# Cosine attention and a GELU layer: one scale and its transposing DMA moved ahead of a square

## The chip, the core and the metric

The kernel runs on one core of a Trainium2 chip. Time is device microseconds of one execution; lower is better. The core has five engines that run side by side, each with a queue of its own that is worked off in order: PE (matrix multiply), DVE (vector), ACT (activation functions), POOL (GpSimd) and SP (here it only issues transfers). Transfers run on 16 DMA engines that all queues share. A transfer that SP issues goes into SP's hardware queue (q1 in the profile); one that POOL issues goes into the software queue (q0).

## The reference

```python
q_n = q / (norm(q, axis=-1) + 1e-6)          # q, k, v: (8 batches, 12 heads, 448, 64)
k_n = k / (norm(k, axis=-1) + 1e-6)
scores = q_n @ k_n.T / tau                   # tau = 0.1
attn = exp(scores - max); attn /= sum(attn)
x = (attn @ v) -> (3584 tokens, 768)         # heads side by side
h = x @ w_in                                 # 768 x 2048
g = 0.5 * h * (1 + erf(h / sqrt(2)))         # exact GELU
out = g @ w_out                              # 2048 x 768
```

All inputs and the output are float32.

## The kernel before

**Tiling.** Four heads of one batch make a quad; a batch has three quads (`NQ = 3`), so there are 24. A quad is computed at a time: its q and k lie as `qk` [128, 2 (q, k), 2 (head pairs), 7, 64] in float32. For each quad the kernel squares q and k (`square`, line 140, POOL), sums the squares of each row (`reduce`, 151, DVE), takes logarithm and exponential of a half for the root (`logs` 162 and `roots` 167, ACT), adds 1e-6 and takes the reciprocal (`inverses`, 176, POOL then DVE for the quad of this change), multiplies q and k by it into bfloat16 (`scale`, 193, two POOL instructions), and turns the result so that the head dimension lies on partitions (`transposes`, 207). For the first batch's quads the turning is done by PE and copied by DVE; from the second batch on it is one transposing DMA issued by SP (line 213).

**Attention.** `scores` (227) multiplies k by q into `st`, `exps` (238) takes the exponential on ACT, `sums` (247) and `values` (261) are PE's row sums and products with v. The sums are turned into a factor on DVE (`turned` 275, `inverted` 280, `spread` 296), and `normalise` (301) multiplies it into `x`, one of six slices of 64 x 2 columns for each call. The last two slices of a batch come from its quad 2.

**The two layers.** `first(b)` (595) is the first layer of a batch with its GELU: 16 tiles `hp` of six contraction steps each, 96 matmuls (line 607), each tile finished by a GELU on ACT (638). The first five tiles start with four steps each (`ahead`), which need only the slices of quads 0 and 1; the other two steps need the slices of quad 2. The tiles take turns on the PSUM banks of attention: two double banks and two single ones, each free again when its GELU has read it. The second layer (`second_pieces`, 323) is cut into single matmuls that the next batch's attention uses as filling between its scores.

**What sets the order.** Everything is issued in an order written out by hand, under `manual_schedule`; each engine runs its part of it in that order, and waits are put in for data and buffers. `attention_first` (385) is the first batch, line by line; `done` counts for each step how many units have been issued, and `upto(f, n)` issues those that are missing. Unit numbers run over the quads with the first quad cut in two, so that unit 4 is quad 0 of the second batch, 5 its quad 1 and 6 its quad 2. Units 5 and 6 share one root, so that `root(5)` needs the squares and sums of both.

**Around the change.** Before, `attention_first` ends with `inverses(4)`, behind the last two slices of `x`. Then `first(0)` issues, behind the first 20 matmuls (lines 617 to 619):

```python
        if b == 0:
            upto(square, nu + 3)
        for n in (nu + 1, nu + 2) if b else (nu + 1,):
            upto(scale, n)
            upto(transposes, n)
```

With `nu = 4` these are the square of unit 6, the scale of unit 4 and its transposing DMA. Next come two loads of `wo` (`load_wo`, issued by POOL), the sums of squares of units 5 and 6, and the 16 GELUs. After the sixth GELU ACT changes its table and works out the root of units 5 and 6 (line 641); POOL then scales both and SP issues their transposing DMAs, with loads of `qk` between. At the end of `first(0)`, `group(1, 0)` issues the first scores of the second batch, which read what the DMA of unit 4 wrote.

Of the kernel before, what the change touches and what calls it, by code (L numbers as in the profile page):

```python
# [16 lines left out]
def kernel(  # L17
# [78 lines left out]
    def mm_tile(name, shape=(128, 512), dtype=F32, aside=None):  # L96
        t = ps_mm.tile(list(shape), dtype, tag=f"mm{turn[0] if aside is None else turn[0] ^ aside}", name=name)
        if aside is None:
            turn[0] ^= 1
        return t  # L100
# [75 lines left out]
    def inverses(n):  # L176
        sr = sr_t.pop(n)
        shape = [128] + shapes[n]
        se = nrm.tile(shape, F32, tag="se", name=f"se{n}")
        if n <= NQ:  # L180
            nc.vector.tensor_reduce(se.rearrange("p j i s c -> p (j i s c)"), sr, mybir.AxisListType.X, ALU.add)
        else:
            nc.gpsimd.tensor_scalar(se, sr, 1e-6, None, ALU.add)  # L183
        rn = nrm.tile(shape, F32, tag="rn", name=f"rn{n}")
        nc.vector.reciprocal(rn, se)  # L185
        rn_t[n] = rn
# [6 lines left out]
    def scale(u, parts=None):  # L193
        g, s0, s1 = units[u]
        n, j = place[u]
        rn = rn_t[n][:, j]
        if g not in qkb_t:
            qkb_t[g] = qkbp.tile([128, 2, C, 2, D], BF16, tag="qkb", name=f"qkb{g}")
        qkb, t = qkb_t[g], qk_t[g]
        for eng, i in parts or ((nc.gpsimd, 0), (nc.gpsimd, 1)):  # L200
            eng.tensor_tensor(  # L201
                qkb[:, i, :, s0:s1].rearrange("p c s d -> p s c d"), t[:, i, s0:s1],
                rn[:, i].to_broadcast([128, s1 - s0, C, D]), ALU.mult)
# [3 lines left out]
    def transposes(u, i=None):  # L207
        g, s0, s1 = units[u]
        qkb = qkb_t[g]
        if g not in qkT_t:  # L210
            qkT_t[g] = qkTp.tile([128, 2, C, 128], BF16, tag="qkT", name=f"qkT{g}")
        if i is None:
            nc.sync.dma_start_transpose(out=qkT_t[g].rearrange("p i c s -> p (i c) s"),
                                        in_=qkb.rearrange("p i c s d -> p (i c s d)"))
            return
        tp = tp_t[u, i] = mm_tile(f"tp{u}_{i}", (128, C, 128), BF16)
        for c in range(C):
            nc.tensor.transpose(tp[64 * s0:64 * s1, c, :], qkb[:, i, c, s0:s1].rearrange("p s d -> p (s d)"), ident)  # L218
# [42 lines left out]
    def values(g, chunks=range(C), aside=None):  # L261
        for c in chunks:
            if c == 0:
                bank_t[g, 0] = ps_acc.tile([128, 512], F32, tag="o", name=f"o{g}_0")
                bank_t[g, 1] = mm_tile(f"o{g}_1", aside=aside)
            for s in range(2):
                for h in range(2):
                    rows, cols = slice(64 * h, 64 * (h + 1)), slice(64 * s, 64 * (s + 1))
                    nc.tensor.matmul(bank_t[g, h][cols, :S], lhsT=v_t[g][rows, s, c, :],  # L269
                                     rhs=pt_t[g, s, c][rows], start=(c == 0), stop=(c == C - 1),  # L270
                                     tile_position=(64 * h, 64 * s))
# [8 lines left out]
    def inverted(g):  # L280
        tr = bank_t.pop((g, "tr"))
        if g < NQ:
            su = tr[:, :, :, 0]
        else:


            for j in range(4):
                o = j ^ 1
                nc.vector.tensor_reduce(tr[32 * j:32 * (j + 1), :, :, 1], tr[32 * o:32 * (o + 1), :, :, 0:1],  # L289
                                        mybir.AxisListType.X, ALU.add)  # L290
            su = rcp.tile([128, 2, NB], F32, tag="su", name=f"su{g}")
            nc.vector.tensor_reduce(su, tr[:, :, :, 0:2], mybir.AxisListType.X, ALU.add)
        rc = bank_t[g, "rc"] = rcp.tile([128, 2, NB], F32, tag="rc", name=f"rc{g}")
        nc.vector.reciprocal(rc, su)

    def spread(g, h):
        rs = rcp.tile([128, NB, 32], F32, tag=f"rs{h}", name=f"rs{g}_{h}")
        nc.vector.transpose(rs, bank_t[g, "rc"][:, h].to_broadcast([128, NB, 32]))  # L298
        rs_t[g, h] = rs.rearrange("p b r -> p (b r)")

    def normalise(g, h):
        b, n = divmod(g, NQ)
        nc.vector.tensor_tensor(x_t[b][:, 2 * n + h, :], bank_t.pop((g, h))[:, :S], rs_t.pop((g, h)), ALU.mult)  # L303
# [68 lines left out]
    done = {}  # L372
# [12 lines left out]
    def attention_first():  # L385
# [154 lines left out]
        roots(4)  # L540
        inverted(2)
        spread(2, 0)
        values(2, (2,))
        values(2, (3,))
        values(2, (4,))
# [2 lines left out]
        normalise(2, 0)  # L548
        spread(2, 1)
        normalise(2, 1)  # L550
        inverses(4)
        done.update({square: 6, reduce: 5, root: 5, scale: 4, transposes: 4})

    passes = [(n, c) for n in range(NQ) for c in range(C)]

# [105 lines left out]
    for b in range(B):  # L661
        if b == 0:
            attention_first()
        else:
            attention(b, fill)
        first(b)
        sb, hf = divmod(b, 2)
        todo = [(t, ni) for t in (range(3) if hf == 0 else range(3, 7)) for ni in range(2)]
        if b == 0:
            todo.sort(key=lambda x: x[1])  # L670
        tail = [2 * S // 128 - 1] if b == B - 1 else []
        fill = [f for t, ni in todo if t not in tail for f in second_pieces(sb, t, ni)]
        fill += [f for t in tail for f in last_pieces(sb, t)]
# [37 lines left out]
```

## Time and profile before

| what | us |
|---|---|
| time, median of 7 | 430.2 (427.87 to 433.18) |
| the profiled execution | 427.87 |
| its span, first to last instruction | 425.9 |
| PE busy | 414.7 (97%) |
| ACT busy | 247.4 (58%) |
| DVE busy | 191.6 (45%) |
| POOL busy | 166.4 (39%) |

The granted TensorE clock is full over the whole span. Times in the views are counted from the first instruction, so they fit into the span; what the time has over it lies around the span. In a timeline a line gives start, length, engine, line of the kernel, operation, what it writes and reads, and how many of one kind were merged; brackets hold the idle time before it and what ended it. The page's list of transfers gives 4.0 us as the median of the transposing DMAs from issue to landing, over 21 of them.

### The profile page before, as it was taken

The page shows a single profiled execution, that of the slowest core. Times are in us where ns is not written, and L with a number is a line of the kernel's source. Part 1 is how long each engine was busy: PE and PEld are TensorE (multiplying, and loading weights), DVE is VectorE, ACT ScalarE, POOL GpSimd, SP SyncE. Part 2 cuts the span into 40 slices and gives each one's busy share as a digit, 9 for nine tenths or more (in the row PEclk, how much of TensorE's full clock was granted, in tenths as well). Part 3 has the DMA queues.
Part 4 walks back from the last instruction along what each step waited for, and adds up shares of the span by engine and source line. Part 5 has one row for each costly group of instructions (what it writes and reads, how often), then busy time and mean ns, then how long its engine had stood idle before and what let it go on. Part 6 is the DMA issues. An engine that isn't in the chain of part 4 may idle for free.

```text
span 425.9 us, 8166 instructions
## 1 busy us (share of the span) xinstructions
PE 414.7 (97%) x3448; PEld 208.5 (49%) x3448; DVE 191.6 (45%) x379; ACT 247.4 (58%) x356; POOL 166.4 (39%) x113
## 2 busy tenths in 40 slices
PE   7899879999999999999999999999999999999996
PEld 3444434555454554545454544555544455445564
DVE  6897017840288304941167501971048611562021
ACT  5895758546655467734767348745666357754300
POOL 5798606360813509090540906353180622000000
PEclk9999999999999999999999999999999999999999
DMA  8999999482492805655092642938076320320023
GB/s 287 270 251 204 190 232 261 97 201 76 84 210 51 229 33 104 168 118 180 17 218 73 133 164 24 239 74 232 2 120 186 82 43 2 82 56 20 2 74 75
DMA packets 68340, 54.99 MB, mean 129 GB/s; under 512 B 40400, under 2 KB 63312, under 8 KB 68304
## 3 DMA queue, kind: packets, MB, share of 16 engines
q1 hardware_dynamic: 55808, 42.25, 37.7%
q0 software_dynamic: 12112, 11.80, 18.0%
q8 instruction: 27, 0.44, 0.4%
q10 hardware_dynamic: 384, 0.43, 0.3%
q14 instruction: 9, 0.07, 0.1%
HBM read 45.61 MB, written 11.01 MB: 133 GB/s over the span
## 4 chain that ended last, share of the span: by engine, by line
PE 90%; DMA 4%; POOL 3%; issue 2%; ACT 0%; DVE 0%; POOLq 0%
PE op L332 35%; PE hp L607 31%; PE st L234 9%; PE o L269 8%; PE sm L258 4%; DMA qkT<-qkb 4%; POOL qkb L201 2%; PE op L347 1%; POOL wi L361 1%; PE sm L253 1%; POOL sq L149 1%; ACT g L638 0%; POOL v L134 0%; PE tp L218 0%; DVE last L350 0%
## 5 line engine op out<-in xcount | busy, mean ns | idle before, releaser
L241 ACT ACTIVATE pt<-st 128x896 bf16<-128x896 f32 x168 | 145.0, 914 | 51.8 <-PE st L234 51.6
L332 PE MATMUL op<-wo,g 128*128 128x384 bf16 x864 | 151.5, 327 | 0.0
L607 PE MATMUL hp<-x,wi 128*128 128x448 bf16 x768 | 146.7, 353 | 0.0
L638 ACT ACTIVATE g<-hp 128x448 bf16<-128x448 f32 x128 | 66.5, 545 | 95.5 <-PE hp L607 95.2
L332 PEld LDWEIGHTS <-g 128*128 128x128 bf16 x864 | 79.3, 98 | 66.9 <-issue 19.1
L607 PEld LDWEIGHTS <-wi 128*128 128x128 bf16 x768 | 74.5, 98 | 71.5 <-issue 2.9
L201 POOL TENSOR_TENSOR qkb<-qk,rn 128x896 bf16<-128x896 f32 (+1 forms) x48 | 77.9, 1649 | 9.2 <-DVE rn L185 9.2
L149 POOL TENSOR_TENSOR sq<-qk 128x1792 f32<-128x1792 f32 (+2 forms) x23 | 67.8, 2950 | 15.1 <-DMA qk<-in_k_dram 14.8
L336 DVE COPY ot<-op 128x384 f32<-128x384 f32 x54 | 29.6, 548 | 89.4 <-PE op L332 89.4
L183 POOL TENSOR_SCALAR se<-sr 128x28 f32<-128x28 f32 (+1 forms) x14 | 4.4, 312 | 167.0 <-ACT sr L174 167.0
L158 DVE TENSOR_REDUCE nq<-sq 128x28 f32<-128x1792 f32 (+2 forms) x30 | 48.7, 1633 | 27.3 <-POOL sq L149 27.2
L234 PE MATMUL st<-qkT 64*64 64x448 bf16 x672 | 52.9, 361 | 4.2 <-DMA qkT<-qkb 3.3
L185 DVE RECIPROCAL rn<-se 128x28 f32<-128x28 f32 (+2 forms) x18 | 6.9, 386 | 89.4 <-POOL se L183 89.2
L269 PE MATMUL o<-pt,v 64*64 64x448 bf16 x672 | 37.8, 352 | 0.0
L234 PEld LDWEIGHTS <-qkT 64*64 64x64 bf16 x672 | 17.6, 104 | 34.0 <-issue 24.7
L298 DVE STREAM_TRANSPOSE rs<-rc 128x448 f32<-128x448 f32 x48 | 28.2, 624 | 0.8
L303 DVE TENSOR_TENSOR x<-o,rs 128x448 bf16<-128x448 f32 x48 | 27.0, 598 | 0.4 <-PE o L269 0.2
L269 PEld LDWEIGHTS <-v 64*64 64x64 bf16 x672 | 18.3, 106 | 17.2 <-issue 9.1
L277 DVE STREAM_TRANSPOSE tr<-sm 128x448 f32<-128x448 f32 x24 | 15.5, 647 | 11.7 <-PE sm L258 11.1
L258 PE MATMUL sm<-pt,ones 128*32 128x448 bf16 x294 | 19.6, 355 | 0.0
L289 DVE TENSOR_REDUCE tr<-tr 32x28 f32<-32x28 f32 x84 | 16.5, 196 | 1.6
L258 PEld LDWEIGHTS <-ones 128*32 128x32 bf16 x294 | 6.9, 95 | 10.1 <-issue 6.6
(44 smaller groups left out, 117.8 us busy)
## 6 DMA issues: line engine op xcount, KB each, us to landing
out_dram<-ot SPq DMA_DIRECT2D x54, 192.0 KB, 2.7
qk<-in_q_dram SPq DMA_DIRECT2D x23, 448.0 KB, 5.7
qk<-in_k_dram SPq DMA_DIRECT2D x23, 448.0 KB, 6.4
v<-in_v_dram POOLq DMA_DIRECT2D x7, 672.0 KB, 9.6
wi<-in_moe_w_in_dram POOLq DMA_DIRECT2D x8, 384.0 KB, 10.5
wo<-in_moe_w_out_dram POOLq DMA_DIRECT2D x4, 768.0 KB, 14.1
qk<-in_q_dram SPq DMA_DIRECT2D x2, 224.0 KB, 3.5
v<-in_v_dram POOLq DMA_DIRECT2D x1, 448.0 KB, 7.9
```

The costliest lines, as they stand in the source:

```text
L149: eng.tensor_tensor(sq[:, part], t[:, part], t[:, part], ALU.mult)
L158: nc.vector.tensor_reduce(nq[:, part], sq[:, part], mybir.AxisListType.X, ALU.add)
L201: eng.tensor_tensor(qkb[:, i, :, s0:s1].rearrange("p c s d -> p s c d"), t[:, i, s0:s1], rn[:, i].to_broadcast([128, s1 - s0, C, D]), ALU. ...
L234: nc.tensor.matmul(st[cols, n, :S], lhsT=qkT[rows, 1, c, cols], rhs=qkT[rows, 0, :, cols], start=True, stop=True, tile_position=(64 * s, 6 ...
L241: nc.scalar.activation(pt[:, :m], st[:, :m, :S], AF.Exp, scale=inv_tau)
L258: nc.tensor.matmul(bank_t[g, "sm"][r:r + 32, :S], lhsT=ones, rhs=pt_t[g, s, c], start=(c < 2), stop=(c >= C - 2), tile_position=(0, r))
L269: nc.tensor.matmul(bank_t[g, h][cols, :S], lhsT=v_t[g][rows, s, c, :], rhs=pt_t[g, s, c][rows], start=(c == 0), stop=(c == C - 1), tile_po ...
L298: nc.vector.transpose(rs, bank_t[g, "rc"][:, h].to_broadcast([128, NB, 32]))
L332: nc.tensor.matmul(ps[:, :NH], lhsT=g_t[sb][:, kf, t * 128:(t + 1) * 128], rhs=wo[:, kf, ni * NH:(ni + 1) * NH], start=(kf == 0), stop=(kf ...
L336: nc.vector.tensor_copy(ot[:, ni * NH:(ni + 1) * NH], ps[:, :NH])
L607: nc.tensor.matmul(hps[m], lhsT=wi[:, kd, m * 128:(m + 1) * 128], rhs=x_t[b][:, kd, :], start=(kd == 0), stop=(kd == KD - 1))
L638: nc.scalar.activation(g_t[sb][:, m, hf * S:(hf + 1) * S], hps.pop(m), AF.Gelu)
```

## The change

The reciprocal of unit 4 goes up, ahead of the last two slices of `x`; the scale of unit 4 and its transposing DMA go with it, and so come ahead of the square of unit 6 on POOL. `first(0)` then finds them issued and leaves them out. Nothing else moves and nothing that is computed changes.

```diff
         roots(4)
         inverted(2)
         spread(2, 0)
+        inverses(4)
+        scale(4)
+        transposes(4)
         values(2, (2,))
         values(2, (3,))
         values(2, (4,))
...
         normalise(2, 0)
         spread(2, 1)
         normalise(2, 1)
-        inverses(4)
-        done.update({square: 6, reduce: 5, root: 5, scale: 4, transposes: 4})
+        done.update({square: 6, reduce: 5, root: 5, scale: 5, transposes: 5})
```

## The prediction

> **What bounds the kernel now.** First the page's busy shares: PE 97% of a 425.9 us span, DVE 45%, ACT 58%, POOL 39%. The change moves POOL, DVE and SP work only, so it can pay only where PE stands still. Hence the waits of PE next: its longest is one wait of 3.3 us of the scores (`st`, line 234) for `qkT`, and no other after the start-up is over 0.3 us. The chain that ended last goes through the same place:
>
> ```profile
> 38.58 1.91 ACT g L638 x5
> 40.48 14.98 DMA qkT<-qkb
> 55.51 0.57 PE st L234 x8
> ```
>
> Start, length, piece. One transposing DMA, here called T4 (quad 0 of the second batch), takes 14.98 us to land, and the scores start the moment it has. The timeline of PE shows the size of the gap:
>
> ```profile
> 33.83 18.33 PE L607 MATMUL hp<-x,wi 128*128 128x448 bf16 x96
> 55.51 0.57 PE L234 MATMUL st<-qkT 64*64 64x448 bf16 x8 [3.35 <-DMA qkT<-qkb]
> ```
>
> The 96 matmuls of the first layer end at 33.83 + 18.33 = 52.16; 3.35 us are idle. Afterwards PE has no wait of size to the end, so what is saved here reaches the end, and 3.35 us is the most there is. What releases T4 is in the timeline of POOL:
>
> ```profile
> 33.63 0.28 POOL L183 TENSOR_SCALAR se<-sr 128x28 f32<-128x28 f32 x1 [0.95 <-ACT sr L174]
> 33.99 3.17 POOL L149 TENSOR_TENSOR sq<-qk 128x1792 f32<-128x1792 f32 x1
> 37.12 3.33 POOL L201 TENSOR_TENSOR qkb<-qk,rn 128x896 bf16<-128x896 f32 x2
> 40.40 1.85 POOL L368 DMA_DIRECT2D wo<-in_moe_w_out_dram  x2
> ...
> 44.38 6.62 POOL L201 TENSOR_TENSOR qkb<-qk,rn 128x896 bf16<-128x896 f32 x4 [0.62 <-DVE rn L185]
> ```
>
> Square of quad 2 (3.17), then the two scales of quad 0, done at 40.45; T4 is issued 0.03 later. SP's queue is otherwise idle then.
>
> **Part 1: the reciprocal moves up on DVE.** DVE's timeline:
>
> ```profile
> 33.91 0.65 DVE L298 STREAM_TRANSPOSE rs<-rc 128x448 f32<-128x448 f32 x1
> 34.66 0.62 DVE L303 TENSOR_TENSOR x<-o,rs 128x448 bf16<-128x448 f32 x1
> ...
> 35.94 0.62 DVE L303 TENSOR_TENSOR x<-o,rs 128x448 bf16<-128x448 f32 x1
> 36.48 0.32 DVE L185 RECIPROCAL rn<-se 128x28 f32<-128x28 f32 x1
> ```
>
> The reciprocal (0.32) now follows the first spread (33.91 + 0.65 = 34.56). Its input `se` is there at 33.63 + 0.28 = 33.91, so it adds no wait: it runs from about 34.60 to 34.92. Behind it are two `x`, a spread and the reduces. The last `x` goes from 36.56 to 36.9. Who waits: the first layer's last two contraction steps. PE starts at 33.83 with five tiles of four steps, 20 matmuls of 18.33 / 96 = 0.191, so it asks for these `x` at 37.65. Cover 0.75 us: cost nothing. Without cover it would be 0.33 us.
>
> **Part 2: POOL's order.** `se` still ends at 33.91. POOL now idles until the reciprocal: 34.92 plus 0.09 (the later pair, 43.79 + 0.50 to 44.38) = 35.0. Scales 3.33: done at 38.34; T4 issued at 38.37, **2.11 us earlier**. The square follows, 38.34 to 41.5, 4.3 us later than before; the two `wo` issues run 41.5 to 43.35, 1.1 later. The software queue has `wo`'s first half and a `v` load ahead of these, so their packets start no later (that queue never empties between 30 and 59 us), and PE needs that half of `wo` only after 48 matmuls, at about 66.
>
> **Part 3: what is late because the square is late.** Reduce of quad 2 on DVE waits for the square: 41.5 + 1.98 = 43.5. The logarithm on ACT waits for it, and ACT's GELUs are queued behind:
>
> ```profile
> 42.70 0.34 ACT L165 ACTIVATE lq<-nq,tiny 128x56 f32<-128x56 f32 x1
> ...
> 44.64 2.43 ACT L638 ACTIVATE g<-hp 128x448 bf16<-128x448 f32 x5
> 47.66 0.54 ACT L638 ACTIVATE g<-hp 128x448 bf16<-128x448 f32 x1 [0.59 <-PE hp L607]
> ```
>
> ACT had nothing to wait for at 42.70; now it starts at 43.55, 0.85 late. The five GELUs end at 47.92 instead of 47.07. The fifth frees the bank of the thirteenth tile, which PE starts at 33.83 + 72 x 0.191 = 47.57: PE stalls 0.35 to 0.4 us, and the first layer ends at about 52.55. That lies inside the gap while T4 lands later; if T4 came first it would be paid. It puts the ceiling of the gain at 55.51 - 52.55 = 2.95 us. The exps of the new scores wait for a table load (1.28 after the last GELU, so to 54.4), with 3.1 us of second-layer matmuls between, so they hold nobody.
>
> **Part 4: how long T4 takes.** Two things make it slow, seen in the DMA view for 43 to 44.5 us, then for 44.5 to 46 us (packets, MB, share of 16 engines; q0 is the software queue, q1 SP's):
>
> ```profile
> q0 software_dynamic: 361, 0.29, 123.7%
> ...
> q1 hardware_dynamic: 3, 0.00, 0.4%
> ```
>
> ```profile
> q0 software_dynamic: 217, 0.19, 94.0%
> q1 hardware_dynamic: 188, 0.05, 37.8%
> ```
>
> T4's packets start only at about 44.5, 4.0 us after its issue, and from then go one for one with the software queue's. A transposition at 85.66 with nothing beside it begins within 1.3 us and lands after 4.0. Here is a rule to weigh: the Trainium skill, DMA: Bandwidth & Descriptors, "Latency and other measured facts", puts the first byte of a hardware-generated DMA at some 600 ns. By it (an estimate) T4 would start at 39.0, be through before PE is, and the gain would be the ceiling, 2.95. By the row it starts at 38.37 + 4.0 = 42.4, amid the same `wo` packets. I take the row: same DMA, same traffic, 2 us apart.
>
> From there it needs as long as before, except that it meets more of `v`: what went by between about 43.4 and 44.5, some 200 packets (q0 moved 361 in 1.5 us). From 49 to 52 us, beside `wo`, q1 moved 560 packets, 187 per us; beside `v` 171 (46 to 47), or 144 over 44.5 to 47 with an instruction fetch in it. So 200 x (1/171 - 1/187) = 0.1 to 200 x (1/144 - 1/187) = 0.3; I take 0.2. Landing: 55.46 - 2.11 + 0.2 = 53.55, so the scores start **1.9 us** earlier.
>
> **Part 5: the next transposition, T5 (quad 1).** Issued at 47.74, it landed 13.6 us later, 61.3; PE asks for it some 8.3 us after the first scores, so before at 63.8, now at 61.9. Its scale is 0.85 later, issue 48.6. Kept at 13.6 it lands at 62.2, 0.3 late; but it queued behind T4, which is now 2 us sooner out of the way, and the total bytes are the same, so about 61. I take no cost; ends 0 and 0.3.
>
> **Sum**: 425.9 - 1.9 = 424.0 of span; with 427.87 - 425.9 = 2.0 around it, 426.0 for the profiled execution. That one was the fastest of those shown, 2.3 under the median, so on the median 430.2 - 1.9 = **428.3**. Bounds of the likeliest: start delay 3.1 to 4.5, hence gain 2.95 down to 1.2, that is 427.25 to 429.0.
>
> **Rivals.**
> A fuller release: T4's late start came of the `wo` issues on POOL at 40.40, or of what was already in the engines then, and is shorter at 38.4. For it: the 1.3 us of the quiet case. Against: loads of later batches beside a `v` stream also start late (at 117.72 one is issued, by 120.8 one packet is out). Gain 2.95: 427.25.
>
> No gain: T4 started just as the first half of `wo` ran out; if that is what it waits for, issuing sooner changes nothing. For: the coincidence at 44.5. Against: the later loads beside `v` start before that stream ends. Time 430.2 + 0.1 (more `v` beside it): 430.3.
>
> Slower: the late square. Through reduce and logarithm it blocks ACT, whose GELUs free PE's banks. With ACT d us late the first layer ends at 52.16 + (d - 0.5); this decides from d = 3.85 (first layer past 55.5) and costs over 0.5% from d = 6.0. My d is 0.85; POOL's scales at their longest row (2.58 instead of 1.67 each) make it 2.7. So it needs some 3.5 us of delay on POOL or DVE that no row shows. At d = 6.4: 432.6.
>
> **How the numbers follow.** Likeliest 0.55, fuller release 0.20, no gain 0.11, slower 0.14. 0.5% is 2.15 us, about what a measurement of this kernel can tell from no change, and the likeliest case lies next to it: of its 0.55 I give 0.26 to faster, 0.28 to same, 0.01 to slower. Fuller release: 0.19 and 0.01. No gain: 0.08 same, 0.03 slower. Slower: 0.13, and 0.01 same. Sums 0.45, 0.38, 0.17. The range reaches past the fuller release by half a microsecond of spread between runs, and past no gain into the slower case: 426.7 to 431.2; the likeliest's own is above.
>
> **What would show it.** Right: T4 issued near 38.4, landing near 53.5 (some 15 us); scale pair at 35.0; square at 38.3; the logarithm at 43.5; PE's wait for `qkT` near 1 us after a first layer ending at 52.5; no wait of PE for T5. Wrong: a landing after 55 in spite of the early issue; a wait before 37.65 for `x`; PE waiting for banks by more than 0.5 us; a new wait of the scores at 61 to 62.

## The result, and the profile after

The changed kernel takes **426.98 us** in the median (426.29 to 431.51, 27 runs), the kernel before, in the same comparison, 429.65 us (64 runs); the ratio is **0.9945, 95% interval 0.9931 to 0.996**, a gain of 2.4 us (1.7 to 3.0). The profiled executions differ by less: spans 425.9 and 424.4, 1.5 us. That gap between 1.5 and 2.4 is the interesting part, and the profiles of before and after alone don't explain it.

PE's wait for the transposing DMA went from 3.3 us to 1.5, and there is a second, short one now. The timeline of PE places them:

```profile
33.51 18.55 PE L609 MATMUL hp<-x,wi 128*128 128x448 bf16 x96
53.55 0.57 PE L234 MATMUL st<-qkT 64*64 64x448 bf16 x8 [1.48 <-DMA qkT<-qkb]
...
62.19 0.38 PE L234 MATMUL st<-qkT 64*64 64x448 bf16 x4 [0.26 <-DMA qkT<-qkb]
```

This execution reached the first layer 0.32 us sooner than the one before (33.51, not 33.83), which is start-up and not the change; so times are compared from the first layer's start. The first scores come 20.04 us behind it instead of 21.68: 1.64 won at T4. The second half of the scores that used to be one piece at 63.51 now waits for T5, and the matmuls behind it start 62.50 - 33.51 = 28.99 behind the layer's start, where it was 64.01 - 33.83 = 30.18: 1.19 is left. T5 took back 0.45. The 1.19 and the 0.32 of start-up are the 1.5 us between the two spans.

POOL, in the new order:

```profile
33.31 0.28 POOL L183 TENSOR_SCALAR se<-sr 128x28 f32<-128x28 f32 x1 [0.95 <-ACT sr L174]
34.54 3.33 POOL L201 TENSOR_TENSOR qkb<-qk,rn 128x896 bf16<-128x896 f32 x2 [0.95 <-DVE rn L185]
37.84 3.17 POOL L149 TENSOR_TENSOR sq<-qk 128x1792 f32<-128x1792 f32 x1
40.96 1.84 POOL L368 DMA_DIRECT2D wo<-in_moe_w_out_dram  x2
```

It idles 0.95 us for the reciprocal, scales, and squares afterwards. T4 is issued at 37.90. On DVE the reciprocal and the two slices of `x` behind it:

```profile
34.17 0.28 DVE L185 RECIPROCAL rn<-se 128x28 f32<-128x28 f32 x1
34.75 0.62 DVE L303 TENSOR_TENSOR x<-o,rs 128x448 bf16<-128x448 f32 x1 [0.29 <-DVE rn L185]
...
36.03 0.62 DVE L303 TENSOR_TENSOR x<-o,rs 128x448 bf16<-128x448 f32 x1
```

The last `x` is there at 36.65; PE asks for it at 33.51 + 20 x 0.191 = 37.33. ACT:

```profile
43.09 0.34 ACT L165 ACTIVATE lq<-nq,tiny 128x56 f32<-128x56 f32 x1 [0.71 <-DVE nq L158]
...
45.03 2.86 ACT L640 ACTIVATE g<-hp 128x448 bf16<-128x448 f32 x6
```

The logarithm now waits 0.71 us for the late sum, and the GELUs come that much later; PE's first layer takes 18.55 us instead of 18.33.

T4's start is in the DMA view for 41 to 42 and for 42 to 43 us, SP's queue (packets, MB, share of the 16 engines):

```profile
q1 hardware_dynamic: 9, 0.00, 1.7%
```

```profile
q1 hardware_dynamic: 180, 0.05, 34.9%
```

It starts at 42.0, again 4.1 us after its issue. It lands 15.6 us after it (53.5), and T5 14.0 us after its own (62.1).

### The profile page after: what moved, and what is told of

Read it like the earlier page. It is cut to its first block, busy times and chain, and to the rows that moved or that the text cites. A ratio compares the mean times of both kernels' runs of the same rounds, so it can differ in the third digit from the quotient of the medians.

```text
span 424.4 us, 8166 instructions
## 1 busy us (share of the span) xinstructions
PE 414.8 (98%) x3448; PEld 208.6 (49%) x3448; DVE 191.7 (45%) x379; ACT 247.3 (58%) x356; POOL 166.4 (39%) x113
## 4 chain that ended last, share of the span: by engine, by line
PE 86%; POOL 5%; DMA 3%; issue 2%; DVE 2%; ACT 0%; POOLq 0%
PE op L332 33%; PE hp L609 30%; PE st L234 9%; PE o L269 8%; PE sm L258 4%; DMA qkT<-qkb 3%; POOL qkb L201 3%; POOL sq L149 1%; PE op L347 1%; DVE nq L158 1%; POOL wi L361 1%; PE sm L253 0%; DVE x L303 0%; POOL v L134 0%; DVE rn L185 0%
## 5 line engine op out<-in xcount | busy, mean ns | idle before, releaser
L149 POOL TENSOR_TENSOR sq<-qk 128x1792 f32<-128x1792 f32 (+2 forms) x23 | 67.8, 2950 | 15.1 <-DMA qk<-in_k_dram 14.9
L234 PE MATMUL st<-qkT 64*64 64x448 bf16 x672 | 53.1, 361 | 2.5 <-DMA qkT<-qkb 1.7
L269 PEld LDWEIGHTS <-v 64*64 64x64 bf16 x672 | 18.3, 106 | 17.2 <-issue 9.1
L289 DVE TENSOR_REDUCE tr<-tr 32x28 f32<-32x28 f32 x84 | 16.5, 196 | 1.6
```

The costliest lines, as they stand in the source:

```text
L149: eng.tensor_tensor(sq[:, part], t[:, part], t[:, part], ALU.mult)
L234: nc.tensor.matmul(st[cols, n, :S], lhsT=qkT[rows, 1, c, cols], rhs=qkT[rows, 0, :, cols], start=True, stop=True, tile_position=(64 * s, 6 ...
```

## The experiments

### E1: the reciprocal alone

```diff
         spread(2, 0)
+        inverses(4)
         values(2, (2,))
...
         normalise(2, 1)
-        inverses(4)
```

> Only the reciprocal of unit 4 moves up (part 1 of the prediction); scale and transposing DMA stay behind the square. My theory: the last slice of x is 0.33 us later, inside a cover of 0.75 us, so PE's 96 first-layer matmuls start and end as before and T4 is issued as before: ratio 1.000, within 0.2%. Rival (the reciprocal itself helps or hurts, by what DVE or POOL does around it): a ratio off 1.000 by more than 0.3%, with a gap in the first layer, or a POOL row that moved.

Measured: 429.47 us, ratio 0.9992 (0.9973 to 1.001). The reciprocal by itself costs and wins nothing: DVE idles 0.29 us behind it as in the changed kernel, and the first layer takes 18.33 us. But this profile showed what the first two had not. PE:

```profile
55.18 0.57 PE L234 MATMUL st<-qkT 64*64 64x448 bf16 x8 [3.49 <-DMA qkT<-qkb]
55.69 4.78 PE L332 MATMUL op<-wo,g 128*128 128x384 bf16 x18
```

and the same kernel by stretches (window, length, busy time and number for PE, PE's loads, DVE, ACT, POOL, then the granted clock, DMA share, GB/s):

```profile
54.00:56.00 2.00, 0.82 (x10) 0.35 (x11) 0.00 (x0) 0.38 (x1) 0.00 (x0) 1.00 1.29 191
56.00:58.00 2.00, 2.00 (x9) 0.98 (x7) 0.00 (x0) 1.34 (x2) 0.00 (x0) 0.53 1.27 191
58.00:60.00 2.00, 2.00 (x10) 0.94 (x8) 0.00 (x0) 0.00 (x0) 0.00 (x0) 0.62 1.32 164
```

Behind the wait for T4 the TensorE clock falls to little over half for some 4 us (0.53 and 0.62). The 18 matmuls take 4.78 us, where they took 3.10 in the profile before: 1.7 us that no wait shows.

### E2, E3: the second half of `wo` loaded behind all three scales

Before and changed kernel, each with:

```diff
-        else:
-            upto(load_wo, 4)
...
                     upto(scale, n)
                     upto(transposes, n)
+                if b == 1:
+                    upto(load_wo, 4)
```

> The kernel before with the second half of wo loaded later: its two loads are issued behind the three scales and transposing DMAs instead of ahead of them. My theory (T4 is slow because its packets alternate with the software queue's): T4 is still issued at 40.4 and still starts about 4 us later, but from about 48 us on it is alone and lands near 51.5, before the first layer ends at 52.2; PE's 3.35 us wait goes without the change: ratio about 0.992. T5, issued into a quiet queue, lands about 4 us after its issue. Rival (the latency is the transposing DMA's own here, or that of the first one): T4 lands 15 us after issue again, ratio 1.000.

> The changed kernel with the same later loads. My theory: T4 lands near 50 us, so the first layer sets the scores, at about 52.4 (the late square costs PE 0.2 us): the change is worth nothing any more, ratio 0.992 to 0.993 to the kernel before and equal to the other kernel with late loads within 0.2%. Rival (the change pays through something else than T4's landing): still some 0.5% faster than that kernel.

Measured: E2 425.78 us, ratio 0.9908 (0.9886 to 0.9929); E3 427.14 us, 0.994 (0.9919 to 0.9961). In neither profile does PE wait for T4 at all. T5, issued when the software queue had all but run dry, landed 4.0 us after its issue in E2 and 4.1 in E3: the 14 us of the other kernels are not the transposing DMA's own. The price of loading so late is seen in E3's timeline of PE:

```profile
35.87 18.55 PE L611 MATMUL hp<-x,wi 128*128 128x448 bf16 x96
54.36 0.57 PE L234 MATMUL st<-qkT 64*64 64x448 bf16 x8
...
70.74 1.46 PE L332 MATMUL op<-wo,g 128*128 128x384 bf16 x8 [0.85 <-DMA wo<-in_moe_w_out_dram]
```

and in E2's profile PE waits for `wo` twice, by 7.3 us together. But that profile is of the longest of E2's six executions, 438.23 us, which the ratio leaves out; how long the other executions waited there isn't known.

Neither profile is a clean pair with the kernel before, since both reach the first layer late: E2's at 37.89, with the clock at 0.66 from 10 to 20 us, E3's at 35.87 at full clock. T4 landed 7.4 us after its issue in E2 and 12.8 in E3, but E2's was issued at 44.55, by when the loads ahead of it were further along, and E3's landing at 53.1 missed the 50 that I had expected, by more than the late start of 2.0 us. The 0.3% between E2 and E3, which I had expected to be 0.2% at most, isn't explained. So the two show for T5 that a quiet software queue takes the delay away; for T4 a better place for `wo` was needed (E7, E8).

### E4: the square of unit 6 twice

```diff
         if b == 0:
             upto(square, nu + 3)
+            square(nu + 2)
```

> The changed kernel with the square of unit 6 done twice (same values again), which puts 3.17 us more on POOL between T4's scales and everything behind. This prices the slower rival (late square, late logarithm, GELUs late, PE without banks). My sum: logarithm 4.0 us later than in the kernel before, first layer ends 3.5 us later, at about 55.7, while T4 still lands at 53.5; the scores start about as in the kernel before: ratio 1.000 (0.998 to 1.002). Were POOL's lateness hidden, it would stay at 0.9945; were it paid in full twice, 1.005.

Measured: 429.79 us, ratio 0.9995 (0.9972 to 1.0017). PE:

```profile
33.38 13.79 PE L609 MATMUL hp<-x,wi 128*128 128x448 bf16 x72
50.48 6.31 PE L609 MATMUL hp<-x,wi 128*128 128x448 bf16 x24 [3.31 <-ACT g L641]
56.72 0.57 PE L234 MATMUL st<-qkT 64*64 64x448 bf16 x8
```

The chain of part 3 is there as predicted: the thirteenth tile waits 3.31 us for a GELU, and the scores wait for the first layer and no more for T4. The ratio came out as summed, but partly by luck, since the sum lacked a term: the clock fell in this wait too (0.59 from 50 to 52 us, 0.56 from 52 to 54), so that the last 24 matmuls took 6.31 us and the scores started at 56.7, where 55.7 had been expected; and behind the scores, where E1 lost its time to the clock, this kernel lost none.

### E5: the kernel before, a second profile

> The kernel before itself, for a second profile: the one of before is of an execution at 427.9 us, while most lie near 429.5. The first set suggests why: with a wait of 3.49 us for T4 the granted TensorE clock fell to 0.53 to 0.62 for some 4 us and 18 matmuls took 4.78 us instead of 3.10. Theory (clock drop): a typical execution of the kernel before shows PE's wait for T4 again at 3.3 to 3.5 us, and behind it a clock near 0.55 and 1.7 us lost. Rival (T4 lands later in the typical execution): a wait of about 5 us and a clock of 1.00.

This one execution took 430.58 us. PE's timeline and two of its stretches:

```profile
55.39 0.96 PE L234 MATMUL st<-qkT 64*64 64x448 bf16 x8 [3.28 <-DMA qkT<-qkb]
56.29 5.52 PE L332 MATMUL op<-wo,g 128*128 128x384 bf16 x18
```

```profile
56.00:58.00 2.00, 2.00 (x10) 0.86 (x7) 0.00 (x0) 1.73 (x2) 0.00 (x0) 0.50 1.27 191
58.00:60.00 2.00, 2.00 (x8) 0.89 (x7) 0.00 (x0) 0.00 (x0) 0.00 (x0) 0.50 1.33 151
```

T4 was issued at 40.44 and landed 14.9 us later, and PE waited 3.28 us, as in the first profile (40.48, 15.0, 3.35). The rival, a later landing, is out for this execution. What differs is the clock: 18 matmuls in 5.52 us instead of 3.10 and the scores in 0.96 instead of 0.57, 2.8 us in all. The times of the kernel before say how often: of the 64, 12 lie at 428.1 or under and 52 at 428.9 or over. The profile that the prediction was made from (427.87) is one of the 12. That the two groups are the clock's doing is seen in the mean clock of each execution. E1's profiled execution, with its one fall, has 0.996, E5's longer fall makes 0.992, and the first profile has 1.000. Of the 32 executions of the kernel before that were timed beside E6b, the five at 427.9 or under have a mean clock of 1.000; of the 27 at 429.1 and over, 26 have 0.996 or less and one has 1.000.

### E6: dummy matmuls in the wait

```diff
             nc.scalar.preload_act_table_set(EXP_SET)
+            if b == 0:
+                spin(8)
             group(b + 1, 0)
```

> The kernel before with eight dummy matmuls (results unused) ahead of the first scores of the second batch, inside the wait for T4, so that PE never stands still for over 3 us. Nothing else moves. Theory (clock drop): T4 lands as before and the wait's end stays, but the clock stays at 1.00: the 1.7 us go in the executions that had them, median near 427.8, ratio 0.995 to 0.997. Rival (the clock has no part in it): ratio 1.000.

Measured: 428.07 us, ratio 0.9946 (0.9925 to 0.9966); five of six executions at 427.7 to 428.5, with mean clocks of 0.999 and 1.000. The one that was profiled is the sixth, 429.43, with 0.996:

```profile
51.82 1.68 PE L383 MATMUL spin<-blank,ident 128*128 128x448 bf16 x8
55.41 0.57 PE L234 MATMUL st<-qkT 64*64 64x448 bf16 x8 [1.91 <-DMA qkT<-qkb]
55.91 4.78 PE L332 MATMUL op<-wo,g 128*128 128x384 bf16 x18
```

Even with only 1.91 us of standing still the clock fell (0.69 from 56 to 58 us, 0.50 from 58 to 60). So the wait was filled further, with `spin(13)` in the kernel before (E6b) and, by the same edit, `spin(4)` in the remaining wait of the changed kernel (E6c):

> The kernel before with thirteen dummy matmuls in the wait for T4 instead of eight: they fill it up to about 54.6, so that less than 1 us of standing still is left. In the profile with eight of them 1.91 us were left and the clock still fell to 0.50. Theory (the clock falls on too little work in a stretch of a few us, not only on a full stop of 3.3): no execution falls any more, median 427.5 to 427.8, ratio 0.994 to 0.996, all executions within 1 us; scores still start at 55.4. Rival (a fall there comes at random, whatever PE does): part of the executions still at 429.4.

> The changed kernel with four dummy matmuls in its remaining wait of 1.5 us. Theory: its executions at 428 and above are those in which the clock fell in this wait; they go, the others stay at 426.3 to 427.3, so median about 426.6, ratio 0.9925 to 0.994, and 1.0 to 1.3 us below the kernel before with the wait filled, which is what the earlier landing of T4 is worth without the clock. Rival (the whole gain of the change is the clock): equal to the kernel before with the wait filled.

Measured: E6b 427.86 us, ratio 0.9967 (0.9949 to 0.9986), 20 of 22 executions at 427.3 to 428.5 with mean clocks of 0.998 and over; E6c 426.81 us, ratio 0.9941 (0.992 to 0.9962), all 11 at 426.4 to 428.0. E6b's two others are at 432.3 and 432.7 (0.984 both); the profile fell on one of these:

```profile
57.38 2.62 PE L383 MATMUL spin<-blank,ident 128*128 128x448 bf16 x13
60.35 0.57 PE L234 MATMUL st<-qkT 64*64 64x448 bf16 x8 [0.35 <-DMA qkT<-qkb]
60.86 3.10 PE L332 MATMUL op<-wo,g 128*128 128x384 bf16 x18
```

All of it is 5 us late, and most of that is the clock, which had fallen in the start-up (0.59 over 10 us is, by estimate, 4 us):

```profile
10.00:20.00 10.00, 8.43 (x41) 3.33 (x41) 7.33 (x13) 6.76 (x10) 4.68 (x6) 0.59 1.15 278
```

At the wait itself it holds: 3.10 us for the 18. The rival (falls at random) is out for this place: none of 22 lies between 428.6 and 432, where the kernel before has the bulk of its executions.

E6c against E6b is the change with the clock taken out: 426.81 to 427.86, **1.05 us** (1.1 by the two ratios). E6b against the kernel before (429.71 in this comparison) is the clock: **1.85 us** between the medians; by the ratio, which counts the two late executions in, 1.4 us (0.6 to 2.2). E6c's profile has T5's wait of 0.69 us in it:

```profile
53.59 0.57 PE L234 MATMUL st<-qkT 64*64 64x448 bf16 x8 [0.64 <-DMA qkT<-qkb]
54.09 3.10 PE L332 MATMUL op<-wo,g 128*128 128x384 bf16 x18
...
62.66 0.38 PE L234 MATMUL st<-qkT 64*64 64x448 bf16 x4 [0.69 <-DMA qkT<-qkb]
```

### E7, E8: the second half of `wo` between the scales of units 5 and 6

The cause points to a better kernel: give the transposing DMAs a quiet queue, and load the weights in time all the same. In the kernel before (E7) and the changed one (E8):

```diff
-        else:
-            upto(load_wo, 4)
...
                 upto(scale, nu + 2)
                 upto(transposes, nu + 2)
+                upto(load_wo, 4)
                 upto(load_qk, 2 * NQ + 1)
```

> The kernel before with the second half of wo issued between the scale of unit 5 and that of unit 6, so earlier than in the kernel with late loads, where PE waited for wo. Theory: T4 starts 4 us after its issue at 40.4, has no wo beside it from about 48 us on and lands by 52; no wait of PE for T4 and none for wo: ratio 0.990 to 0.991. Rival (wo's packets come back soon enough to slow T4): a wait of over 1 us left, ratio 0.994.

> The same place for wo in the changed kernel. Theory: T4 lands before the first layer ends, and the change has nothing left to win; its late square costs PE 0.2 us of waiting for a bank: ratio 0.9905 to 0.992, equal to the kernel before with wo in the middle or up to 0.1% slower. Rival (the change pays by itself, whatever the loads do): 0.5% faster than that kernel.

Measured: E7 **424.73 us, ratio 0.9873 (0.985 to 0.9896)**; E8 424.86 us, ratio 0.9905 (0.987 to 0.9939). PE in E7, then in E8:

```profile
34.01 18.33 PE L607 MATMUL hp<-x,wi 128*128 128x448 bf16 x96
52.27 0.57 PE L234 MATMUL st<-qkT 64*64 64x448 bf16 x8
52.77 3.10 PE L332 MATMUL op<-wo,g 128*128 128x384 bf16 x18
```

```profile
33.58 18.55 PE L609 MATMUL hp<-x,wi 128*128 128x448 bf16 x96
52.06 0.57 PE L234 MATMUL st<-qkT 64*64 64x448 bf16 x8
```

No wait for T4, for T5 or for `wo` is left in either. T4 in E7, issued at 40.66 as in the kernel before, lands after 9.8 us instead of 15.0; that is what the second half of `wo` had cost it. Without this traffic the change has nothing to win: E8 is not faster than E7 in time, and its first layer bears the 0.22 us of the late square (18.55 against 18.33). In E8 T4 is issued sooner (37.97) and still lands later, 13.9 us after its issue: 18.3 us behind the start of the first layer, where E7 has 16.5, and only 0.3 us ahead of the layer's end. Why it takes so long there was not tried. Two of E8's nine executions, at 429.4 and 429.8, lift its ratio; why they are late was not looked into, and the two medians are 0.13 us apart. E7 is better than I expected (0.990 to 0.991), and the clock fits as the reason: the wait of 3.35 us and a fall worth 1.85 make 5.2 of its 5.4 us. Both kernels beat the two that were compared.

## Why the prediction was right, and where it was not

The forecast was 428.3 from 430.2, a gain of 1.9 us; measured are 2.4 us, inside the range and on the forecast side. But that the sizes are this close is luck: two terms of the sum are wrong in opposite ways.

**What bounds the kernel now: the clock was left out.** "3.35 us is the most there is" took the wait for its whole cost. The profile read was of one of the rarer executions in which the clock held; I had noted that it lay 2.3 us under the median, and put the 2.3 us down to nothing. E5 shows that the wait is the same in a typical execution and that behind it the clock falls to 0.50; E6b prices that at 1.85 us in the median. The Trainium skill has a rule for it, in TensorE: Matmul & The Clock Gate, "What's actually happening": TensorE goes to half its clock after at least one window of about 3.4 us in which it idles, and the windows run freely, without a new start when a kernel begins. Taken to the letter, a wait of 3.35 us is just too short to fill a window and costs nothing more; so close to the edge, the fall should have been priced all the same. The runs agree with the half clock (0.50), and at almost the same wait some executions keep the clock and some don't (12 of 64 kept it). They don't agree with the need for a whole idle window: the clock fell behind 3.28 us (E5), 3.31 (E4) and 1.91 (E6). What condition it follows is not shown. The changed kernel's 1.48 us were short enough: 25 of its 27 executions have a mean clock of 0.998 or more, and the other two (430.2 and 431.5) have 0.984, as E6b's profile has, whose fall lay in the start-up; where theirs lay was not profiled. The three at 428.1 to 428.6 have 1.000, so they are late by something else.

**Parts 1 to 3 held.** Counted from the first layer's start, the scale pair was forecast at 35.0 (found 34.54, which is 34.86 on the scale of the profile before), T4's issue at 38.37 (38.22), the logarithm at 43.55 (43.41), no wait for `x` (none; E1 confirms the cost of nothing), a bank stall of 0.35 to 0.4 us (0.22). E4 confirms the chain of the slower rival; in the change itself it stayed as short as summed. (By the rival's own formula the time at d = 6.4 is 432.75, not 432.6; nothing rests on it.)

**Part 4, row against rule, held.** T4's start delay was taken from the row, 4.0 us, and not from the 600 ns of the Trainium skill (DMA: Bandwidth & Descriptors, "Latency and other measured facts"): 4.1 in the profile after. With it fall the rivals "fuller release" (no shorter at 38) and "no gain" (its packets start at 42.0, while `wo`'s go on beside them). What follows was under-sized: T4 landed 15.6 us after its issue, where 15.2 had been summed, so 1.64 us were won and not 1.9. Which of its packets' neighbours made the 0.4 us was not tried.

**Part 5 failed in size.** T5 was to cost nothing, 0.3 us at most; it cost 0.45, and one of the prediction's own signs of being wrong, a new wait of the scores at 61 to 62, came up (at 62.19). The step that failed is "the total bytes are the same, so about 61". The second half of `wo`, issued 0.9 us later in the new order on the same scale, ended later. From 58 to 60 us the software queue moved, before and after:

```profile
q0 software_dynamic: 180, 0.13, 40.6%
```

```profile
q0 software_dynamic: 358, 0.27, 85.8%
```

From 60 to 61 it moved 2 packets before and 74 after. T5, issued 0.7 us later on the same scale (48.13 + 0.32, not 47.74), had this traffic beside it for longer, took 14.0 us instead of 13.6 and landed at 62.1. No run varied this alone.

**The sum as it should have been**: 1.64 at T4, less 0.45 at T5, makes 1.19 in the profile and 1.05 in time (E6c against E6b). To this comes the clock, which the kernel before loses behind its wait and the changed kernel does not: 1.85 us between medians, 1.4 by the ratio. The changed kernel's own median is 0.17 us above E6c's, too little to tell from nothing. Together that is 2.5 us by the ratios and 2.9 by the medians, where 2.4 by the ratio and 2.7 by the medians were measured. About half of the gain or more, then, is one that the prediction does not have.

## What to carry to other kernels

A wait of PE of around 3 us can cost more than its length, and in only part of the executions: before summing, ask whether the profiled execution is a typical one, and compare its time with the median. A transfer that lands late may be late because of its neighbours; moving a big load that nobody needs yet out of its way gave 5.4 us (E7's ratio). Less 1.85 for the clock that is some 3.5, over three times the 1.05 that issuing the transfer sooner gave. And when one transfer of a queue is brought forward, look at the next one: here it took back 0.45 of 1.64 us.

## What the runs showed that was not expected

- The TensorE clock fell to 0.50 behind a wait of 3.28 us and behind one of 1.91 us, and stayed at 1.00 behind one of 3.35 us in another execution of the same kernel. It came back after some 3.4 to 5.6 us, by estimate (twice the 1.7 us lost in E1 and the 2.8 lost in E5).
- T4, issued beside a busy software queue, moved its first packets 4.0 us after its issue before the change and 4.1 after it. T4 and T5 landed after 13.6 to 15.6 us in these two kernels and after 9.4 to 9.8 in E7; with the queue quiet T5 took 4.0 to 4.1 us in all (E2, E3).
- The clock can fall in the start-up too (0.59 from 10 to 20 us in E6b's profile, 0.66 in E2's); the first layer starts 5.4 and 4.1 us late there. A late start alone doesn't show it: E3's is 2.0 us late at full clock.
